# Fourier mixing and a low-rank mixer MLP on one core: wider x-stationary products on four column tiles, loads without overlap, low-rank rows by products of their own

## The chip, the core and the metric

The kernel runs on one core of a Trainium2 chip. The metric is the device time of one execution in microseconds. Six runs of the kernel before gave a median of 494.63 us (490.86 to 497.08). The engines are named as in the profile: PE (matmul; PEld is its weight load), DVE (vector), ACT (scalar), POOL (GpSimd), SP (the engine that issues most DMAs).

## The reference

The input `x` has 8 sequences of 3136 rows of 256 numbers. The real part of a two-dimensional Fourier transform (over the rows and over the 256 columns) goes into a mixer layer:

```python
X = np.fft.fft(np.fft.fft(x, axis=1), axis=2).real
xt = X.transpose(0, 2, 1)
h = xt @ U @ V                      # U: 3136 x 32, V: 32 x 3136
u = X + h.transpose(0, 2, 1)
out = u + np.maximum(u @ w_ch1, 0.0) @ w_ch2    # 256 -> 1024 -> 256
```

## The kernel before

The 3136 rows are factored as 49 x 64 (`N1`, `N2`), so the row transform has a 49-point stage and a 64-point stage; by symmetry 25 of the 49 frequencies (`NK1`) are computed. The transform of the 256 columns is folded into the weights (`W1p`, `W1m`, `W2`, `Bp`, `Bm`) and into sums and differences of mirrored columns. The eight sequences run as four pairs.

**The first pair** is treated apart. Its two sequences are loaded one at a time by `load_single` (L108), as bf16, into one tile `X` of 98 partitions x 32 lines x 256 columns: odd partitions hold lines 33 to 63, even partitions the lines 31 down to 0. The pool of that tile has a single buffer, so the second sequence cannot be loaded before the last product of the first has read it. Line 32 goes to `x32`. The last of the big loads (two rows, issued at L124) writes a row that the loads of L121 and L122 have also written; the framework therefore makes POOL wait for those loads before it issues this one and everything behind it on its queue.

The 49-point stage with x stationary is `turned_products` (L206). For each of 128 column pairs (d and 256-d) and for each of the two line halves c (lines 0 to 31 of one kind and of the other) it loads a 98 x 32 slice of `X` as weights and streams 50 columns of the table `Fs`. The four outputs of a step lie on four column tiles (32 partitions each): two columns d and 64+d, two halves. `turned_out` (L225) copies PSUM to the tile `g` with one instruction of 63 partitions for each column half h. `line32` and `row32` add row 63 by a DMA from a small tile. The framework keeps order between all writes into `g`, so the copies of DVE and ACT run one after another. For the first sequence this happens in four rounds of 16 columns (L581 to L584, PSUM pool `psh`), for the second in eight steps of 8 columns (`turned_steps`, PSUM pool `psd` of two buffers) that lie among the MLP's work.

**Low-rank part.** `te_single` (L278) forms U^T times the row-transformed data from `g`; `te_out` casts it to the tile `te`, and `spread` copies `te` into partitions 64 to 127 of `g` for every one of the 25 frequencies. The 64-point stage `s3_steps` (L299) then multiplies `g` (128 partitions: 64 of data, 64 of low-rank rows) with the table `T`, whose partitions 64 to 127 hold V and a mirrored V; it writes `q`.

**Front.** Before the first product, tables are made: index patterns on POOL (iotas), angles on DVE, sines on ACT. T's row 63 comes by a DMA from `trow` (L452), which POOL fills; the mirror copy of T (L576) waits for it, and it stands ahead of the `g` copies on DVE. The tables `residual_tables` (L409) are made on DVE ahead of `te_out`. `keep_warm` runs matmuls on zeros.

**The MLP.** A chunk is up to 512 tokens; there are 13 a pair, with 4 slots each. In a slot PE runs `mlp1` of the current chunk (two 128-wide hidden blocks, 4 matmuls of 512 columns into one PSUM tile of `psh`), ACT turns it to bf16 with a relu (hT, L360), PE runs `mlp2` of the chunk before (8 matmuls L369 and 2 L372). Every second slot ACT copies half of the output (om, L378), DVE makes sum and difference (L379, L380) and SP issues four output DMAs (L384). `plan` (L676) places all other work by hand in these slots: the first sequence's remaining `s3` steps in slots 1 to 8, the second sequence's turned steps in slots 4 to 11, its `te_single` in slot 15, the next pair's loads from slot 8 on. [...]

Of the kernel before, what the change touches and what calls it, by code (L numbers as in the profile page):

```python
# [22 lines left out]
def kernel(  # L23
# [84 lines left out]
    def load_single(b):  # L108

        X = zpool.tile([P, 32, D], BF16, tag="z", name="X")  # L110
        nc.vector.memset(X[0:PR, 31, :].bitcast(FP32), 0.0)
        nc.vector.memset(x32[b][:].bitcast(FP32), 0.0)
        yield X
        r0, L = b * N1, N1 - 1

        def rows(lo, n, line, step, o):
            src = bass.AP(x.tensor, x.offset + ((r0 + lo) * N2 + line) * D, [[N2 * D, n], [step * D, o.shape[1]], [1, D]])
            nc.gpsimd.dma_start(out=o, in_=src)

        rows(0, L, 33, 1, X[1:2 * L:2, 0:31, :])  # L120
        rows(0, L, 31, -1, X[0:2 * L:2, 0:16, :])  # L121
        rows(0, L, 15, -1, X[0:2 * L:2, 16:32, :])  # L122
        rows(L, 1, 33, 1, X[PR - 1:PR, 0:31, :])
        rows(L - 1, 2, 31, -1, X[PR - 4:PR:2, 0:32, :])  # L124
        nc.gpsimd.dma_start(out=x32[b][0:PR:2], in_=x_pn[r0:r0 + N1, 32, :])

# [79 lines left out]
    def turned_products(X, ps, i0, n):  # L206

        for i in range(n):
            if i % 8 == 0:
                first = [True] * 4  # L210
            for m in range(2):
                for h in range(2):
                    d = 64 * h + i0 + i
                    for c in range(2):
                        o = ps[64 * h + 32 * c:64 * h + 32 * c + 32, i]
                        w = X[0:PR, :, (256 - d if d else 128) if m else d]
                        if d:
                            f = Fs[:, 0:3:2 if m else 1, c, 0:NK1] if m else Fs[:, 0:2, c, 0:NK1]
                            oc = o[:, :, 0:NK1]
                        else:  # L220
                            f, oc = Fs[:, 0, c, 0:NK1], o[:, m, 0:NK1]
                        nc.tensor.matmul(oc, w, f, start=first[2 * h + c], stop=True, skip_group_check=True)  # L222
                        first[2 * h + c] = False

    def turned_out(g, ps, i0, n, evacs):  # L225
        for h in range(2):
            d0 = 64 * h + i0
            evacs[h](g[0:63].rearrange("p k (s d) -> p s k d", s=2)[:, :, :, d0:d0 + n],
                     ps[64 * h:64 * h + 63].rearrange("p i s k -> p s k i")[:, :, 0:NK1, :])

    def turned_steps(pr, b, X, evacs):
# [3 lines left out]
        def step(r):  # L235
            if r == 0:
                row32(g, line32(b))
            ps = psd.tile([P, 8, 2, 32], FP32, tag="ps", name="ps")
            turned_products(X, ps, 8 * r, 8)
            turned_out(g, ps, 8 * r, 8, evacs)  # L240
# [58 lines left out]
    def s3_steps(pr, b, evac):  # L299
# [4 lines left out]
        def mm(o, k1, blk, st):  # L304
            lt = pr.g[b][:, k1, blk::2]
            r = T[:, k1, 0:64] if k1 == 0 else T[:, k1, :].rearrange("p (s j) -> p s j", s=2)
            nc.tensor.matmul(o, lt, r, start=st, stop=True, skip_group_check=True)  # L307

        def step(g, blk):
            ps = psd.tile([P, 2, 256], FP32, tag="ps", name="ps")  # L310
            k0 = 4 * g
            for u in range(4):
                us = slice(u * 64, (u + 1) * 64)
                mm(ps[:, 0, us] if k0 + u == 0 else ps[:, :, us], k0 + u, blk, u == 0)
# [15 lines left out]

        for g in range(6):
# [30 lines left out]
    def mlp2(ch, t):  # L362
        q, nt = ch.pr.q, len(ch.units) // 2
        if t % 2 == 0:
            ch.po = pso.tile([P, 2, 2, P], FP32, tag="o", name="ops")
        ps = ch.po[:, t % 2]
        tk = slice(ch.c0 + t * P, ch.c0 + (t + 1) * P)
        for j in range(JT):
            nc.tensor.matmul(ps, ch.h[:, j, t * P:(t + 1) * P], W2[:, j, :], start=(j == 0 and t % 2 == 0),  # L369
                             stop=(j == JT - 1), skip_group_check=True)  # L370
# [3 lines left out]
        if t % 2 == 1 or t == nt - 1:  # L374
            n = t % 2 + 1
# [5 lines left out]
            for i in range(n):  # L381
                for hf in range(2):
                    b, r0 = ch.units[2 * (t - n + 1 + i) + hf]
                    nc.sync.dma_start(out=out[b].rearrange("(k2 k1) d -> k1 k2 d", k1=N1)[r0],  # L384
                                      in_=ob[hf * 64:(hf + 1) * 64, i])


# [47 lines left out]
    X0 = next(loads)  # L435
    for _ in loads:
# [8 lines left out]
    nc.gpsimd.dma_start(out=w2_f, in_=moe_w_ch2.rearrange("(t p) (s d) -> p t s d", p=P, s=2))  # L445
    for te in tes:
        nc.gpsimd.memset(te[64:128].bitcast(FP32), 0.0)
    trow = tmp([1, NK1, 64], "trow", BF16)
    nc.gpsimd.memset(trow[:], 1.0)
    nc.gpsimd.memset(trow[:, 0::2, 1::2], -1.0)  # L450
    nc.gpsimd.memset(trow[:, 1::2, 0::2], -1.0)
    nc.sync.dma_start(out=T[63:64, :, 0:64], in_=trow[:])  # L452

    Vk = uv.rearrange("p (k2 k1) -> p k1 k2", k1=N1)
    for lo, hi in [(0, 9), (9, 17), (17, NK1)]:
        nc.gpsimd.tensor_copy(T[64:96, lo:hi, 0:64], Vk[64:96, lo:hi, :])

# [23 lines left out]

    pv = tmp([PR, 10], "pv")
    h = ph[0:PR]
    u, m = tmp([PR, 1], "u"), tmp([PR, 1], "m")
    ts(u[:], pf[0:PR], h, 0.5 / 49, AL.subtract, AL.mult)
    ts(pv[:, 0:1], u[:], alt[0:PR, 0:1], None)
    nc.vector.scalar_tensor_tensor(pv[:, 0:1], h, 48.0 / 49, pv[:, 0:1], op0=AL.mult, op1=AL.add)
    for i, off in enumerate([192.0, 192.25, 192.5, 192.75]):
        ts(pv[:, 1 + i:2 + i], h, (0.5 if i < 2 else -0.5), off)
    ans = tmp([PR, 3, 2, 32], "ans")  # L490
    for tab, c, off in [(0, 0, 192.25), (0, 1, 192.5), (1, 0, 1), (1, 1, 2), (2, 0, 3), (2, 1, 4)]:
        ts(ans[:, tab, c, :], jf[0:PR, 0:32], pv[:, 0:1], off if off > 100 else pv[:, off:off + 1])
    mask_bits(ans[:], 16)
    sin_of(Fs[:], ans[:], 16)
    ts(m[:], h, -1.0, 1.0)
    ts(pv[:, 6:7], u[:], 24.0 / 49, m[:], AL.subtract, AL.mult)
    an2 = tmp([PR, 3, 32], "an2")
    for i, off in enumerate([0.25, 0.0, 0.5]):
        ts(pv[:, 7 + i:8 + i], m[:], off, 192.0)
        ts(an2[:, i], jf[0:PR, 0:32], pv[:, 6:7], pv[:, 7 + i:8 + i])  # L500
    mask_bits(an2[:], 16)

    ub = tmp([64, N1, R], "ub", BF16)
    nc.scalar.copy(ub[:].rearrange("p k r -> p (k r)"), U_f)
# [15 lines left out]
    mask_bits(ta[:], 18)  # L522
    ups = psh.tile([P, 2, 512], FP32, tag="h", name="ups")
# [7 lines left out]
    ua = tmp([64, NK1, 64], "ua", FP16)  # L531
    sin_of(F32[:], an2[:], 16)

# [7 lines left out]
    mask_bits(jq[:], 16)  # L543

    sin_of(ua[:], ta[:], 18)
    ts(rv[:, :, :, 1, :], ups_v, -1.0, None)
    pn = tmp([64, 2], "pn")
    ts(pn[:, 1:2], pf[0:64], 32.0, 32.0, AL.is_ge, AL.mult)
    ts(pn[:, 0:1], pn[:, 1:2], pf[0:64], 31.0, AL.subtract, AL.add)
    ts(pn[:, 0:1], pn[:, 0:1], 1.0 / S, None)  # L550
    ts(pn[:, 1:2], pn[:, 1:2], -0.25 / 32, 32.25)
    ta2 = kio.bitcast(FP32)
    ts(ta2, kio, pn[:, 0:1], pn[:, 1:2])
    mask_bits(ta2, 18)
    keep_warm(8)

    for k0, k1 in [(0, 16), (16, 25)]:
        ps = psh.tile([P, 16, 64], FP32, tag="h", name="uups")
        for k in range(k0, k1):
            o = ps[0:64, k - k0]  # L560
            nc.tensor.matmul(o, ua[:, k], ub[:, k].unsqueeze(1).to_broadcast([64, 2, R]),
                             start=((k - k0) % 8 == 0), stop=True, skip_group_check=True)
# [4 lines left out]
        if k0:  # L567
            copy_dve(us[:, k0:k1].rearrange("p k (r s) -> p k s r", s=2), ps[0:64, 0:k1 - k0].rearrange("p k (s r) -> p k s r", s=2))
        else:
            copy_act(us[:, k0:k1].rearrange("p k (r s) -> p k s r", s=2), ps[0:64, 0:k1 - k0].rearrange("p k (s r) -> p k s r", s=2))  # L570
    keep_warm(8)
    sin_of(T[0:63, :, 0:64], ta2[0:63], 18)
    Q = tmp([P, 3, P], "Q", FP32R)
    sin_of(Q[:, 0:2], jq[:], 16)
    nc.scalar.mul(Q[:, 2], Q[:, 1], -1.0)
    nc.vector.tensor_copy(T[0:64, :, 64:128], T[0:64, :, 63::-1])  # L576
# [3 lines left out]
    row32(g0, line32(0))  # L580
    for r in range(4):  # L581
        ps = psh.tile([P, 16, 2, 32], FP32, tag="h", name="tps")
        turned_products(X0, ps, 16 * r, 16)
        turned_out(g0, ps, 16 * r, 16, [copy_dve, copy_act])  # L584
    nc.scalar.copy(T[64:96, 1:9, 64:128], Vk[64:96, 48:40:-1, :])
    nc.vector.tensor_copy(T[96:128, 0:9, 0:64], T[64:96, 0:9, 0:64])
    ts(T[96:128, 1:9, 64:128], T[64:96, 1:9, 64:128], -1.0, None)
    nc.scalar.copy(T[64:96, 9:NK1, 64:128], Vk[64:96, 40:24:-1, :])

    for c in range(2):  # L590
        cs = slice(c * 512, (c + 1) * 512)
        ps = psh.tile([P, 2, 512], FP32, tag="h", name="w1ps")
        for blk in range(2):
            for f in range(2):
# [168 lines left out]
```

## Time and profile before

| quantity | value |
|---|---|
| median of six runs | 494.63 us |
| the profiled execution: its time | 497.14 us |
| the profiled execution: its span | 495.4 us |
| PE busy | 447.8 us (90%) |
| ACT, DVE, POOL busy | 290.6, 224.4, 135.3 us |
| PE busy in 0 to 100 us | 67.4 us |
| PE busy in 100 to 480 us | 372.5 us |
| mean granted PE clock | 0.959 |

The span is the time between the first and the last event of the execution; its device time is 1.74 us longer. A busy time is the time in which an engine has an instruction in work. The table's last rows split PE's busy time: after 100 us PE is hardly ever idle, in the first 100 us it is idle a third of the time.

### The profile page before, as it was taken

The numbers are of one execution on the slowest core, as the hardware profiler recorded it, in microseconds if no ns is written. First come the engines' busy times: TensorE is split into PE (matmuls) and PEld (weight loads), VectorE is DVE, ScalarE is ACT, GpSimd is POOL, SyncE is SP. The second block draws the span as 40 slices with busy tenths as digits, with TensorE's granted clock in tenths as the row PEclk, the third lists the DMA queues.
The fourth block names the chain that finished last, engine by engine and source line by source line (L and its number), as shares of the span: only waits on it lengthen the run. The fifth ranks groups of instructions, "written<-read, shape, count | busy, mean of one in ns | idle before, by whom it ended". The sixth has DMA issues, their size and how long they took to land.

```text
span 495.4 us, 11419 instructions
## 1 busy us (share of the span) xinstructions
PE 447.8 (90%) x4651; PEld 323.3 (65%) x4715; DVE 224.4 (45%) x524; ACT 290.6 (59%) x394; POOL 135.3 (27%) x134
## 2 busy tenths in 40 slices
PE   5655658999999999999999999999999999999993
PEld 2454346766778577777677777776777677766763
DVE  8326413548744353764624437645444344221211
ACT  4315514556775655677765556777746555666661
POOL 2720214358431502644306025336040000000000
PEclk9857958999999999999999999999999999999998
DMA  9430804446765935568649345767493333333423
GB/s 155 108 110 1 124 9 127 127 120 197 223 176 150 193 105 160 152 182 239 184 121 218 80 105 163 214 186 223 111 179 92 66 68 67 69 75 66 95 48 81
DMA packets 59506, 64.02 MB, mean 129 GB/s; under 512 B 13764, under 2 KB 52510, under 8 KB 59326
## 3 DMA queue, kind: packets, MB, share of 16 engines
q1 hardware_dynamic: 49086, 41.61, 36.2%
q0 software_dynamic: 8208, 15.38, 12.9%
q10 hardware_dynamic: 2160, 6.29, 3.4%
q8 instruction: 37, 0.61, 0.5%
q14 instruction: 15, 0.12, 0.1%
HBM read 34.28 MB, written 32.19 MB: 134 GB/s over the span
## 4 chain that ended last, share of the span: by engine, by line
PE 71%; DMA 7%; DVE 7%; issue 4%; ACT 3%; SPq 1%; POOL 1%; DVEq 0%; POOLq 0%; ACTq 0%
PE ops L369 29%; PE hps L358 28%; PE ops L372 4%; PE ps L307 3%; PE ps L222 2%; PE ps L179 2%; ACT hT L360 2%; DMA X<-in_x_dram 2%; DMA xa<-in_x_dram 1%; DMA g<-zturn 1%; DVE q L80 1%; DMA out_dram<-ob 1%; PE teps L269 1%; DMA T<-trow 1%; SPq L384 1%
## 5 line engine op out<-in xcount | busy, mean ns | idle before, releaser
L360 ACT ACTIVATE hT<-hps 128x1024 bf16<-128x1024 f32 (+1 forms) x208 | 202.6, 975 | 127.3 <-PE hps L358 117.8
L369 PE MATMUL ops<-W,hT 128*128 128x256 bf16 x1568 | 226.2, 274 | 1.3 <-DVE W L635 1.1
L369 PEld LDWEIGHTS <-hT 128*128 128x128 bf16 x1568 | 146.0, 98 | 35.1 <-issue 0.6
L379 DVE TENSOR_TENSOR ob<-ops,om 128x256 f32<-128x256 f32 (+1 forms) x100 | 41.9, 419 | 190.5 <-ACT om L378 179.1
L358 PE MATMUL hps<-q,W1p 128*128 128x512 bf16 (+1 forms) x416 | 104.5, 361 | 3.1 <-issue 1.4
L358 PE MATMUL hps<-q,W1m 128*128 128x512 bf16 x353 | 95.6, 379 | 2.0 <-ACT hT L360 0.5
L138 POOL TENSOR_TENSOR y<-xa,xb 98x1020 f32<-98x1020 f32 (+1 forms) x24 | 55.1, 2294 | 122.5 <-DMA xa<-in_x_dram 119.9
L80 DVE CAST q<-ps 128x512 bf16<-128x512 f32 (+3 forms) x120 | 64.5, 559 | 30.4 <-PE ps L307 26.4
L358 PEld LDWEIGHTS <-W1p 128*128 128x128 bf16 x448 | 40.7, 99 | 28.2 <-issue 3.8
L372 PEld LDWEIGHTS <-q 128*128 128x128 bf16 x392 | 38.6, 98 | 22.4 <-issue 2.0
L358 PEld LDWEIGHTS <-W1m 128*128 128x128 bf16 x384 | 35.6, 97 | 26.4 <-issue 1.4
L307 PE MATMUL ps<-T,g 128*128 128x128 bf16 (+1 forms) x400 | 38.0, 222 | 6.3 <-DVE g L291 4.3
L378 ACT COPY om<-ops 128x256 f32<-128x256 f32 (+1 forms) x100 | 36.9, 369 | 9.1 <-PE ops L369 8.5
L380 DVE TENSOR_TENSOR ob<-ops,om 128x256 f32<-128x256 f32 (+1 forms) x100 | 40.9, 409 | 0.0
L372 PE MATMUL ops<-Bp,q 128*128 128x128 f16 x200 | 38.9, 221 | 0.0
L307 PEld LDWEIGHTS <-g 128*128 128x128 bf16 x400 | 30.1, 100 | 11.8 <-DVE g L291 4.5
L372 PE MATMUL ops<-Bm,q 128*128 128x128 f16 x192 | 36.9, 219 | 0.0
L291 POOL COPY g<-te 64x1024 int32<-64x1024 int32 (+1 forms) x21 | 22.5, 1117 | 51.1 <-DVE te L255 45.2
L77 ACT CAST z<-ps 128x512 bf16<-128x512 f32 x48 | 28.2, 588 | 11.0 <-PE ps L179 10.4
L222 PEld LDWEIGHTS <-X 98*32 98x32 bf16 x1024 | 19.9, 172 | 10.8 <-issue 10.4
L103 POOL DMA_INDIRECT xb<-in_x_dram,idx x24 | 24.8, 1033 | 5.4 <-issue 4.5
L129 DVE TENSOR_TENSOR yb<-y 98x508 bf16<-98x508 f32 (+1 forms) x24 | 25.2, 1051 | 0.6 <-POOL y L138 0.6
(132 smaller groups left out, 231.3 us busy)
## 6 DMA issues: line engine op xcount, KB each, us to landing
out_dram<-ob SPq DMA_DIRECT2D x392, 64.0 KB
xa<-in_x_dram SPq DMA_DIRECT2D x24, 392.0 KB
g<-zturn SPq DMA_DIRECT2D x6, 800.0 KB
zturn<-z ACTq DMA_DIRECT2D x9, 512.0 KB
w_f<-in_moe_w_ch_dram POOLq DMA_DIRECT2D x2, 1024.0 KB, 9.3
X<-in_x_dram POOLq DMA_DIRECT2D x4, 384.0 KB, 10.7
X<-in_x_dram POOLq DMA_DIRECT2D x2, 744.0 KB, 8.0
zturn<-z ACTq DMA_DIRECT2D x3, 448.0 KB
```

The costliest lines, as they stand in the source:

```text
L77: nc.scalar.copy(o, i)
L80: nc.vector.tensor_copy(o, i)
L138: nc.gpsimd.tensor_tensor(ck.y[:, 0:n, 1:256], ck.xa[:, 0:n, 1:256], rb[:, :, 255:0:-1], op=AL.add)
L222: nc.tensor.matmul(oc, w, f, start=first[2 * h + c], stop=True, skip_group_check=True)
L307: nc.tensor.matmul(o, lt, r, start=st, stop=True, skip_group_check=True)
L358: nc.tensor.matmul(ps[:, i, 0:n], (W1p if ch.sg > 0 else W1m)[:, blk, j], q[:, blk, c0:c0 + n], start=(blk == 0), stop=(blk == 1))
L360: nc.scalar.activation(ch.h[:, 2 * jp:2 * jp + 2, 0:n], ps[:, :, 0:n], AF.Relu)
L369: nc.tensor.matmul(ps, ch.h[:, j, t * P:(t + 1) * P], W2[:, j, :], start=(j == 0 and t % 2 == 0), stop=(j == JT - 1), skip_group_check=True)
L372: nc.tensor.matmul(ps[:, j], q[:, j, tk], (Bp if ch.sg > 0 else Bm)[:, j], start=False, stop=False, skip_group_check=True)
L378: nc.scalar.copy(om[:, 0:n], ch.po[:, 0:n, 1])
L379: nc.vector.tensor_tensor(ob[:, 0:n, 0:P], ch.po[:, 0:n, 0], om[:, 0:n], op=AL.add)
L380: nc.vector.tensor_tensor(ob[:, 0:n, P:D], ch.po[:, 0:n, 0], om[:, 0:n], op=AL.subtract)
```

## The change

It has six parts.

1. `load_single`: each row of `X` is written by one load only. Two loads of one row each take the place of the single-row load and the two-row load, and `x32` is issued second.
2. The front is put in another order: the angles of `ua` first, then `Fs`, T, `F32`, `Q`; trow by two int32 fills; the mirrored V rows of T by POOL (L491) instead of ACT; the U products in four groups in the PSUM pool `pso`.
3. `turned_products` becomes `quarter_products`: one product with N=100 holds both halves c, on four column tiles that belong to four columns d, 32+d, 64+d, 96+d. `quarter_out` copies each column tile and each half apart, so a PSUM tile takes eight copies, shared in turn by ACT and DVE. The first sequence uses it for 32 of its 128 column pairs, and `half_products` and `half_out` (the old form) in rounds of 8 columns for the rest. The second sequence uses it in all of its eight steps, which move from slots 4 to 11 to slots 6 to 13.
4. The load of the second sequence is issued right after the first sequence's products, ahead of `W1p`, `te_single` and the first `s3` steps.
5. First sequence: the first four `s3` groups multiply only 64 rows of `g`, and the low-rank rows are added by further products with `te` (memset to 128 rows) as weights; `spread` is left to frequencies 8 to 24. `residual_tables` comes after the groups.
6. The last chunk: each token block gets its own PSUM tile and copies, and a part of the output DMAs is issued on ACT's queue.

```diff
-        rows(0, L, 33, 1, X[1:2 * L:2, 0:31, :])
-        rows(0, L, 31, -1, X[0:2 * L:2, 0:16, :])
-        rows(0, L, 15, -1, X[0:2 * L:2, 16:32, :])
-        rows(L, 1, 33, 1, X[PR - 1:PR, 0:31, :])
-        rows(L - 1, 2, 31, -1, X[PR - 4:PR:2, 0:32, :])
-        nc.gpsimd.dma_start(out=x32[b][0:PR:2], in_=x_pn[r0:r0 + N1, 32, :])
+        rows(33, 1, X[1:2 * L:2, 0:31, :])
+        nc.gpsimd.dma_start(out=x32[b][0:PR:2], in_=x_pn[r0:r0 + N1, 32, :])
+        rows(31, -1, X[0:2 * L:2, 0:16, :])
+        rows(15, -1, X[0:2 * L:2, 16:32, :])
+        nc.gpsimd.dma_start(out=X[PR - 1:PR, 0:31, :], in_=x_pn[r0 + L:r0 + N1, 33:64, :])
+        nc.gpsimd.dma_start(out=X[PR - 2:PR - 1, 31::-1, :], in_=x_pn[r0 + L:r0 + N1, 0:32, :])
...
+    def quarter_products(X, ps, i0, n):
+        for i in range(n):
+            for m in range(2):
+                for q in range(4):
+                    d = 32 * q + i0 + i
+                    o = ps[32 * q:32 * q + 32, i]
+                    w = X[0:PR, :, (256 - d if d else 128) if m else d]
+                    if d:
+                        f, oc = Fs[:, 0:3:2 if m else 1, :, 0:NK1] if m else Fs[:, 0:2, :, 0:NK1], o[:, :, :, 0:NK1]
...
+                    nc.tensor.matmul(oc, w, f, start=(i % 4 == 0 and m == 0), stop=True, skip_group_check=True)
+
+    def quarter_out(g, ps, i0, n, evac):
+        for q in range(4):
+            d0 = 32 * q + i0
+            for c in range(2):
+                r = 32 - c
+                evac(g[32 * c:32 * c + r].rearrange("p k (s d) -> p s k d", s=2)[:, :, :, d0:d0 + n],
+                     ps[32 * q:32 * q + r, 0:n, :, c, 0:NK1].rearrange("p i s k -> p s k i"))
...
-            ps = psd.tile([P, 8, 2, 32], FP32, tag="ps", name="ps")
-            turned_products(X, ps, 8 * r, 8)
-            turned_out(g, ps, 8 * r, 8, evacs)
+            ps = psd.tile([P, 4, 2, 2, 32], FP32, tag="ps", name="ps")
+            quarter_products(X, ps, 4 * r, 4)
+            quarter_out(g, ps, 4 * r, 4, evac)
...
+    for r in range(2):
+        ps = psh.tile([P, 8, 2, 2, 32], FP32, tag="h", name="tps")
+        quarter_products(X0, ps, 8 * r, 8)
+        quarter_out(g0, ps, 8 * r, 8, copy_alt)
     for r in range(4):
-        ps = psh.tile([P, 16, 2, 32], FP32, tag="h", name="tps")
-        turned_products(X0, ps, 16 * r, 16)
-        turned_out(g0, ps, 16 * r, 16, [copy_dve, copy_act])
+        i0 = 16 + 32 * (r // 2) + 8 * (r % 2)
...
+        half_products(X0, ps, i0, 8)
+        half_out(g0, ps, i0, 8, [copy_dve, copy_act])
...
+    for ps, (g, blk) in zip(pss, groups):
+        lines(ps, g, blk, 64)
+    for ps, (g, blk) in zip(pss, groups):
+        lines(ps, g, blk, P, tes[0])
+        move(ps, g, blk)
+    spread([(nc.vector, 8, 16)])(g0, tes[0])
...
-            place(turned_steps(cur, 1, X1, [copy_act, copy_dve]), 4, 12)
+            place(turned_steps(cur, 1, X1, copy_alt), 6, 14)
...
+            if not last or t == 0:
+                for i in range(n):
+                    for hf in range(2):
+                        store(i, hf, nc.sync)
+            else:
+                store(0, 0, nc.sync)
+                late.append(lambda: store(0, 1, nc.scalar))
+            while last and late and (t == 1 or t == nt - 1):
+                late.pop(0)()
```

## The prediction

> **What bounds the kernel now.** I read the page's slices first, then busy time by stretches, then the chain of waits, and last the timeline by engine. The stretches (length, then busy PE, PEld, DVE, ACT, POOL, clock, DMA):
>
> ```profile
> 0.00:100.00 100.00, 67.42 (x1358) 47.64 (x1369) 44.52 (x125) 41.10 (x55) 30.79 (x47) 0.81 0.44 95
> 100.00:480.00 380.00, 372.53 (x3228) 269.58 (x3280) 176.84 (x391) 245.67 (x333) 104.54 (x88) 1.00 0.56 140
> ```
>
> From 100 us to 480 us PE is 98% busy at full clock: only work taken off PE would count there, and the change takes none. So the time is to be won or lost in the first 100 us and in the tail. The chain of waits (start, duration, what) shows the two large holes of the front:
>
> ```profile
> 24.50 5.17 DMA T<-trow
> ...
> 29.77 0.58 DVE T L576
> 30.35 0.90 DVE g L80
> 31.28 0.83 ACT g L77
> 32.15 2.54 PE tps L222 x114
> ...
> 52.29 0.53 POOL X L118
> 52.82 7.92 DMA X<-in_x_dram
> 60.74 2.62 issue
> 63.37 0.67 POOL X L118
> 64.04 3.13 DMA x<-in_x_dram
> ```
>
> In the first, PE waits from 27.0 to 32.15 for a copy of g, because DVE stands at T's mirror copy, and that for the trow DMA. In the second, PE waits from 58.9 to 67.2 (8.3 us) for the second sequence: its load starts at 52.3, POOL waits at the overlapping row, and only then x32 is issued. The timeline shows one turned step (ACT, DVE, PE):
>
> ```profile
> 87.95 0.48 ACT L77 CAST g<-ps 63x400 bf16<-63x400 f32 x1 [1.08 <-PE ps L222]
> 88.46 0.58 DVE L80 CAST g<-ps 63x400 bf16<-63x400 f32 x1
> 88.89 1.03 ACT L360 ACTIVATE hT<-hps 128x1024 bf16<-128x1024 f32 x1 [0.46 <-PE hps L358]
> 89.77 1.38 PE L222 MATMUL ps<-Fs,X 98*32 98x50 f16 x64
> ```
>
> DVE starts 0.03 us after ACT's end, although both halves were in PSUM at the same time. The waits answer says the same:
>
> ```profile
> DVE g L80 <- ACT g L77: 18.3, 7, 11.9
> ```
>
> So copies into g run in a chain across the two engines. The tail's copies:
>
> ```profile
> 487.95 0.37 ACT L378 COPY om<-ops 128x256 f32<-128x256 f32 x1 [1.60 <-PE ops L369]
> 488.35 0.42 DVE L379 TENSOR_TENSOR ob<-ops,om 128x256 f32<-128x256 f32 x1 [1.21 <-ACT om L378]
> ```
>
> PE ends at 487.88; SP issues its last 12 output DMAs from 485.19 without a gap to 492.92, 0.64 us each, so the tail ends on SP's queue.
>
> [...] a step has 1.3 us of products and 1.06 us of copies. [...] Here 64 products of N=50 took 1.31 us on the chain (20.5 ns each at full clock), and in 32.15 to 37.41 about 19 ns at clock 0.5; [...] The trace's number is used. [...] I leave 20 ns[...]. [...]
>
> **The change part by part.**
>
> *Load of the first sequence.* POOL no longer waits 11.34 us (the wait ahead of the row at 15.53), so the iota of 1.58 us, V, W1, W2 and trow move up. W2's issue still waits for the first X load (landing 9.5 us after 1.42). Then two fills of 0.5 us: trow is issued at about 13 instead of 24.5 us. W1 and W2 still share the DMA engines, so I keep its 5.17 us: landed at 18.1 (from 15, with 2 us, to 20.5, when W2's bytes are through). Sines and angles are all done by 16. But the U products now lie ahead of the X products on PE, in four groups over the two buffers of pso, and the second group's copy is on DVE behind T's mirror copy: 18.15+0.58, fill 0.17, copy 0.55: 19.4. The fourth group takes 0.4, keep_warm's 8 at 0.2 to 0.43 take about 2.9: the first X product starts at S=22.7, where before it started at 19.6. S is 20.5 to 25 by trow's landing.
>
> *Copies of the first sequence.* Two tiles of 64 products (1.3 us each) come first, with 8 copies of 400 elements each. One pair in the chain costs 0.48+0.57+0.06=1.11, eight pairs 8.9. Four rounds of the old form follow; the second waits for psd (line 32 holds the other buffer): 1.1, then three times 1.33 of PE, then 1.1. Sum: S+1.3+8.9+1.1+4.0+1.1=S+16.4, or 39.1; before, g was full at 39.27. Nothing is won: the time gained on trow's wait goes into smaller copies.
>
> *From g to the first hidden activation.* w1ps 2.9 us on PE to 40.9 (X's products end at 38.0), teps 1.6 to 42.5, te copies 0.6, 64-row products 4x0.43 at cold clock, low-rank products 4x0.43 with copies behind them: q is full at 47.1. On DVE then spread 0.7, T 0.8, residual_tables 2.2 (all as in the trace): 50.8. Bp (0.5) stands ahead of the first hT on ACT: hT starts at 51.3; before, at 51.16. The five us of T, tables and spread that lay ahead of s3 have been moved behind q and are late again at Bp. W2's fold (2.4 us of DVE) is behind them: the first mlp2 at 58.1 instead of 57.6.
>
> *Load of the second sequence.* It starts at 39 (end of the g copies), six issues of 0.65, landed by about 50 to 51. The steps that need it begin at slot 6. The 8.3 us wait is gone; slot 6's hT comes at about 62.3 (58.1, two mlp2 of 1.0, two mlp1 of 0.9, small waits).
>
> *Turned steps, slots 6 to 13.* PE: 32 products of about 20 ns instead of 64, 0.65 us saved a step, 5.2 in all. Copies: 8 of 200 elements instead of 2 of 400. The trace has none of this size. Without any fixed part a copy would take half of 0.48 and 0.58 (0.24, 0.29); if all were fixed, the whole. [...] I take 0.31 and 0.36; te's casts of 129 columns from PSUM (0.29 on DVE) stand near them. The built order has every copy wait for the other engine's last one, so ACT is held for 4x0.31+3x0.36+6x0.035=2.53 us a step, in order ahead of the next hT. A slot then takes ACT 1.03 (hT)+2.53=3.56; in odd slots also om 0.39 and the chain's DVE behind the ob pair, 0.46: 4.41. PE needs 0.86+1.0+0.65=2.5 and waits. Eight slots: 4x3.56+4x4.41=31.9. Extras: q and z32 in slot 6 1.0, q in slot 7 0.7, W1m and Bm in slot 8 1.7, the pair tables in slot 10 1.1: 4.4. So slot 14's hT is at 62.3+36.3=98.6; before it was at 102.40. Gain 3.8: of the 8.3 us wait and 5.2 us of products, more than half is given back as PE waiting for ACT.
>
> *After slot 14.* The same work in the same order on a PE that is full: 0. The next pair's loads keep their slots, and slots 8 to 13 got longer, so DMA isn't later.
>
> *Tail.* The last chunk's SP issues fall from 8 to 5, with the previous chunk's 4 ahead: 485.19+9x0.64=490.95 instead of 492.92. ACT's three are done by 489.6. Gain 2.0 (1 to 2.5).
>
> **Sum.** -0 -3.8 -2.0 = -5.8: span 495.4-5.8=489.6, and 491.3 with the 1.74 us around it. The profiled execution (497.14) was 2.5 slower than the median of the runs; from the median 494.63 I forecast 488.8. Its own range: S from -2.2 to +2.5, chain links 10% either way (3 us), tail 1: 483 to 494.
>
> **The rivals.**
>
> *PE stays the bound in the turned steps.* If the chain were not kept (copies of ACT and DVE side by side) or its links were half as long, slots 6 to 13 take PE's 2.5 us plus the s3 products: about 22 instead of 36.3 us. The gain is 14 more: about 475. For it: ACT was idle half of this stage (17.6 us busy in 37.2 us). Against: the 0.03 us handover, seven times.
>
> *The copies don't shrink (slower).* If a copy of 200 elements on 32 partitions costs as much as one of 400, 0.48 and 0.58, ACT is held 4x0.48+3x0.58+0.2=3.87 a step, and the eight slots take 8x(1.03+0.2+0.23+3.87)+4.4=47. Slot 14 is at 109.4, +7.0, less the tail's 2.0: +5.0, or 499.6. It decides from an average slot of 5.26 us on, where the gains are used up ((102.4+2.0-62.3)/8); I have 4.54. For it: a 1-column DVE operation already takes 0.15 and a 98x32 one 0.20 to 0.33. Against: te's 0.29.
>
> A smaller doubt: PE, with 2.5 us of work in 4 us, may lose its clock. Before, at 43% busy (80.8 to 83.3), it was granted 0.70 in the stretch after. [...] At half clock PE needs about 4.4 us a slot, near ACT's 4.5; that costs up to 4 us, inside my range.
>
> **How the numbers follow.** Forecast 0.62, PE-bound 0.20, copies that don't shrink 0.18. A measurement here tells about 0.5%, or 2.5 us, from no change. Faster by more: 0.8 of the forecast's, all of the second: 0.70. Within: 0.17 of the forecast's and 0.2 of the third: 0.14. Slower: 0.16. The range takes half of each rival: 477 to 497.
>
> **What would show it.** Right: eight ACT-DVE pairs a step at 0.03 us handover, ACT copies near 0.31 and DVE near 0.36, PE idle before mlp1 in slots 7 to 13 and slot distance near 4.5 us; no X wait of PE after 58 us; first hT within 2 us of 51; SP's last issue near 2 us after ACT's. Wrong: a first X product before 20 us, products of N=100 near 40 ns each [...], or a hole after 100 us that wasn't there.

## The result and the profile after

The changed kernel takes 490.36 us (median of 21 runs, 487.84 to 492.1) against 494.3 us for the kernel before on the same chips (42 runs, 490.11 to 497.22): a ratio of 0.9923, 95% interval 0.9906 to 0.9941. That is 3.8 us, or 0.8%: small, but clear of no change. The two profiled spans stand further apart, 489.1 against 495.4 us, because the profiled execution before (497.14 us) lay 2.8 us over its median and the one after (490.88 us) 0.5 us over.

Busy time by stretches, in the same columns as before (length; busy PE, PEld, DVE, ACT, POOL with instruction counts; clock; DMA share; GB/s):

```profile
0.00:100.00 100.00, 63.68 (x1042) 42.07 (x1053) 56.06 (x157) 47.84 (x90) 34.04 (x51) 0.88 0.45 98
100.00:480.00 380.00, 372.19 (x3214) 269.75 (x3263) 175.23 (x392) 246.46 (x335) 103.47 (x86) 1.00 0.57 140
```

After 100 us nothing has changed for PE: 98% busy, as before. In the first 100 us PE is busy less (63.68 us, before 67.42) and idle more, while DVE is busy 11.5 us more and ACT 6.7 us. PE runs 1042 instructions there instead of 1358, DVE 157 instead of 125, ACT 90 instead of 55: the products became fewer, the copies more.

The chain of waits of the changed kernel through the front (start, duration, what):

```profile
15.24 1.70 DVE jq L439 x4
16.96 1.10 DVE jq L428
18.09 0.52 ACT Q L432
...
18.94 0.55 ACT us L77
...
20.37 0.58 ACT us L77
...
22.55 2.77 PE warm L499 x6
25.32 1.13 PE tps L217 x63
26.47 0.49 ACT g L77
26.99 0.57 DVE g L80
...
50.54 0.35 DVE qa L439
...
50.97 0.26 DVE qa L428
...
51.43 0.23 issue
51.67 1.01 ACT hT L381
```

Neither hole of the chain before is there any more, neither the wait of T's copy for trow nor the wait for the second sequence. The new limits are mostly copies and tables: DVE's angles for Q (`jq`), ACT's `us` copies queued behind Q, then the copy pairs into `g`, then the tables of `residual_tables` (`qa`), behind which Bp and the first hidden activation stand on ACT:

```profile
51.25 0.51 ACT L432 ACTIVATE Bp<-qa,pi 128x256 f16<-128x256 int32 x1 [5.00 <-DVE qa L428]
```

That first hT starts at 51.67, before at 51.16. The chain contains no waiting for X.

One of the eight steps in the timeline, as it was shown before:

```profile
90.27 0.32 ACT L77 CAST g<-ps 32x200 bf16<-32x200 f32 x1 [0.42 <-DVE g L80]
...
90.62 0.36 DVE L80 CAST g<-ps 31x200 bf16<-31x200 f32 x1 [0.38 <-ACT g L77]
91.01 0.32 ACT L77 CAST g<-ps 32x200 bf16<-32x200 f32 x1 [0.43 <-DVE g L80]
91.36 1.02 ACT L381 ACTIVATE hT<-hps 128x1024 bf16<-128x1024 f32 x1
91.36 0.37 DVE L80 CAST g<-ps 31x200 bf16<-31x200 f32 x1 [0.39 <-ACT g L77]
91.79 0.71 PE L217 MATMUL ps<-Fs,X 98*32 98x100 f16 x32 [0.69 <-DVE g L80]
92.43 1.03 PE L379 MATMUL hps<-q,W1m 128*128 128x512 bf16 x4
```

The 32 products with N=100 need 0.71 us, half of the 1.38 us that 64 products with N=50 needed. But hT stands on ACT behind the last of its four copies and starts when that ends, 1.2 us after its own products (at 90.1). Each of those copies waits for DVE's copy before it, and PE then waits for a copy too (0.69 us). Over slots 6 to 13 PE is busy 24.5 of 36.35 us. The waits say the same of the whole run (waiting engine and tile, releaser: us in total, times, longest us):

```profile
ACT g L77 <- DVE g L80: 23.3, 35, 1.7
DVE g L80 <- ACT g L77: 18.0, 32, 4.6
```

Before, the second of the two had 18.3 us in 7 times, and the first 12.7 us in 3 times, none of them in the steps. The waits in number went from 10 to 67. The tail in the timeline:

```profile
478.83 7.83 SPq L405 DMA_DIRECT2D out_dram<-ob  x10
...
483.20 0.82 PE L390 MATMUL ops<-W,hT 128*128 128x256 bf16 x6
...
484.61 1.13 ACTq L405 DMA_DIRECT2D out_dram<-ob  x2
```

PE ends at 484.0 and SP's last issue at 486.7; the span ends 5.1 us after PE, where before it ended 7.5 us after it. Counted from the last hT, which takes in the small waits that PE now has in the tail, it is 10.6 us to the end instead of 12.4.

### The profile page after: what moved, and what is told of

The parts are those of the page before. It is cut to its first block, busy times and chain, and to the rows that moved or that the text cites. A ratio compares the mean times of both kernels' runs of the same rounds, so it can differ in the third digit from the quotient of the medians.

```text
span 489.1 us, 10763 instructions
## 1 busy us (share of the span) xinstructions
PE 439.6 (90%) x4280; PEld 314.5 (64%) x4343; DVE 234.0 (48%) x558; ACT 295.4 (60%) x428; POOL 137.5 (28%) x137
## 3 DMA queue, kind: packets, MB, share of 16 engines
q1 hardware_dynamic: 48846, 41.42, 36.7%
## 4 chain that ended last, share of the span: by engine, by line
PE 69%; DVE 13%; ACT 8%; DMA 5%; issue 3%; SPq 1%; DVEq 0%; ACTq 0%
PE ops L390 28%; PE hps L379 27%; PE ps L321 4%; ACT hT L381 4%; PE ops L393 4%; DMA out_dram<-ob 3%; DVE g L80 3%; ACT g L77 2%; PE ps L178 2%; DMA g<-zturn 2%; DVE q L80 2%; SPq L405 1%; DVE ob L401 1%; PE teps L283 1%; DVE ob L400 1%
## 5 line engine op out<-in xcount | busy, mean ns | idle before, releaser
L390 PE MATMUL ops<-W,hT 128*128 128x256 bf16 x1568 | 225.3, 273 | 4.1 <-ACT hT L381 2.8
L390 PEld LDWEIGHTS <-hT 128*128 128x128 bf16 x1568 | 145.3, 98 | 38.2 <-ACT hT L381 3.0
L305 POOL COPY g<-te 64x1024 int32<-64x1024 int32 (+1 forms) x22 | 23.7, 1122 | 60.4 <-DVE te L269 47.4
L321 PE MATMUL ps<-T,g 128*128 128x128 bf16 (+3 forms) x400 | 37.5, 220 | 1.6 <-DMA g<-zturn 0.7
L77 ACT CAST z<-ps 128x512 bf16<-128x512 f32 x48 | 28.2, 587 | 10.6 <-PE ps L178 9.3
L321 PEld LDWEIGHTS <-g 128*128 128x128 bf16 (+1 forms) x400 | 29.7, 99 | 6.8 <-issue 2.0
L128 DVE TENSOR_TENSOR yb<-y 98x508 bf16<-98x508 f32 (+1 forms) x24 | 24.0, 999 | 0.0
L178 PE MATMUL ps<-yb,F 98*128 98x258 bf16 (+1 forms) x108 | 18.9, 265 | 3.0 <-DVE q L80 3.0
```

The source lines that it names most:

```text
L77: nc.scalar.copy(o, i)
L178: nc.tensor.matmul(o[..., cs], F[:, 2 * t + i].rearrange("p b k c -> p (b k c)"), y[..., cs], start=first, stop=True, skip_group_check=True)
```

## The experiments

Each kernel is the changed one with one edit, if nothing else is said. Ratios are to the kernel before, which ran on the same chip with each. The experiments ran on three chips, and the kernel before had medians of 495.62, 494.55 and 492.26 us there; to compare a ratio with the changed kernel's 0.9923 is to take it that both kernels differ alike from chip to chip. Times within the trace are of one profiled execution each; "slot 6 to 14" is the distance of the hT starts of these slots.

| kernel | median us | ratio, 95% interval | first X product | first hT | slot 6 to 14 | span |
|---|---|---|---|---|---|---|
| kernel before | 494.3 | 1 | 19.61 | 51.16 | | 495.4 |
| changed kernel | 490.36 | 0.9923 (0.9906 to 0.9941) | 25.25 | 51.67 | 36.3 | 489.1 |
| steps in the old form | 484.18 | 0.9779 (0.9745 to 0.9814) | 25.27 | 52.08 | 30.9 | 484.0 |
| the steps' copies on DVE alone | 485.47 | 0.9817 (0.9778 to 0.9857) | 23.69 | 50.94 | 28.6 | 482.8 |
| first sequence in the old form | 490.27 | 0.9886 (0.9847 to 0.9925) | 27.03 | 52.06 | 36.4 | 488.9 |
| Bp in slot 3 | 489.67 | 0.9880 (0.9844 to 0.9917) | 24.59 | 48.98 | 36.6 | 488.1 |
| old tail | 492.88 | 0.9952 (0.9931 to 0.9972) | 26.25 | 53.09 | 36.7 | 493.1 |
| load of the second sequence late | 491.67 | 0.9943 (0.9916 to 0.9970) | 23.64 | 50.98 | 36.5 | 488.8 |
| old overlapping loads | 499.21 | 1.0159 (1.0131 to 1.0187) | 33.48 | 60.94 | 36.4 | 496.1 |
| te spread instead of own products | 493.07 | 1.0001 (0.9981 to 1.0021) | 27.02 | 53.96 | 36.3 | 493.1 |
| V casts held back | 488.92 | 0.9893 (0.9848 to 0.9937) | 22.77 | 50.24 | 36.4 | 486.8 |
| three edits together | 479.39 | 0.9755 (0.9727 to 0.9782) | 23.81 | 48.29 | 27.5 | 477.9 |
| four edits together | 476.86 | 0.9713 (0.9675 to 0.9752) | 24.75 | 47.88 | 27.5 | 478.2 |
| before, with the new steps | 499.34 | 1.0107 (1.0062 to 1.0152) | 19.15 | 48.94 | | 496.3 |

The columns of the first X product and the first hT vary without an edit that could move them. The kernel before and the kernel before with the new steps have one and the same front, and their first hT differ by 2.2 us. The two traces part at the first sequence's load: POOL waits 11.34 us at the overlapping row in one and 9.07 in the other, and trow is issued at 24.50 and at 22.27.

### The steps in their old form

```diff
-            ps = psd.tile([P, 4, 2, 2, 32], FP32, tag="ps", name="ps")
-            quarter_products(X, ps, 4 * r, 4)
-            quarter_out(g, ps, 4 * r, 4, evac)
+            ps = psd.tile([P, 8, 2, 32], FP32, tag="ps", name="ps")
+            turned_products(X, ps, 8 * r, 8)
+            turned_out(g, ps, 8 * r, 8, [copy_act, copy_dve])
```

> The changed kernel, with the second sequence's eight steps (slots 6 to 13) in the old form: 64 products of N=50 and two copies of 63 partitions a step, all else as changed. If the chain of eight copies holds ACT and so sets the slot (4.54 us), slots fall to about 3.3 us, as before, and slot 14 comes 8 to 10 us earlier: about 481 us against 490.4 of the changed kernel. If instead PE sets the slots and the halved products are what the change gains, the old form costs 8 x 0.65 = 5.2 us: about 495.5.

The kernel is 1.4% faster than the changed one. Slots 6 to 14 take 30.9 us instead of 36.3, although PE has 64 products a step again instead of 32. A step in its timeline:

```profile
82.36 1.04 PE L404 MATMUL hps<-q,W1p 128*128 128x512 bf16 x4
82.48 0.49 ACT L77 CAST g<-ps 63x400 bf16<-63x400 f32 x1 [0.96 <-PE ps L261]
83.00 0.58 DVE L80 CAST g<-ps 63x400 bf16<-63x400 f32 x1 [0.70 <-ACT g L77]
...
83.44 1.03 ACT L406 ACTIVATE hT<-hps 128x1024 bf16<-128x1024 f32 x1 [0.47 <-PE hps L404]
...
84.32 1.37 PE L261 MATMUL ps<-Fs,X 98*32 98x50 f16 x64
```

ACT is done with its one copy long before PE has finished `mlp1`; hT now waits for PE (0.47 us), not for a copy. From slot 7 on a slot took 3.2 to 5.8 us; the longest lies where PE ran at clock 0.60 (70 to 74 us), the last five took 3.2 to 3.5 us. The old form is the better one: its 0.65 us more of products a step cost less than the six extra copies.

### The eight copies on one engine

```diff
-            place(turned_steps(cur, 1, X1, copy_alt), 6, 14)
+            place(turned_steps(cur, 1, X1, copy_dve), 6, 14)
```

> The changed kernel, with all eight copies of a step of the second sequence on DVE instead of in turn on ACT and DVE. If the hold of ACT by the chain sets the slot, ACT is free, DVE has 8 x 0.36 = 2.9 us and 0.4 to 0.8 us of other work a slot, and a slot takes about 3.6 instead of 4.5 us: 6 to 7 us less, about 484. If the length of the copies one after another sets it, whoever makes them, it stays at 2.9 us plus DVE's own work, and nothing is gained: 490 or a little more.

```profile
85.18 5.97 DVE L80 CAST g<-ps 32x200 bf16<-32x200 f32 x16
```

Sixteen copies without a gap in 5.97 us are 0.37 us each, eight in 2.97 us; the changed kernel needs 2.5 us of chain on ACT for the same data. Slots 6 to 14 shrink to 28.6 us, or 3.57 a slot, although the copies of a step now take longer, because ACT, which hT needs, is free. So it is not the number of copies as such but that they hold the engine of hT. Behind slot 14 DVE is the late one (`te_single` waits for its last copies at 94.85), and a part is given back: slot 14 is 9.2 us earlier than in the changed kernel, the span 6.3.

### The first sequence in its old form

All 128 column pairs in eight rounds of 8 columns, two copies of 400 elements each, over the three PSUM pools. In the changed kernel 64 of the 128 pairs, not 32, are in the wide form: two rounds of 32.

```diff
-    for r in range(2):
-        ps = psh.tile([P, 8, 2, 2, 32], FP32, tag="h", name="tps")
-        quarter_products(X0, ps, 8 * r, 8)
-        quarter_out(g0, ps, 8 * r, 8, copy_alt)
-    for r in range(4):
...
+    for r in range(8):
+        pl_, tg_ = [(psh, "h"), (psd, "ps"), (pso, "o"), (psh, "h")][r // 2]
+        ps = pl_.tile([P, 8, 2, 32], FP32, tag=tg_, name="tps")
+        turned_products(X0, ps, 8 * r, 8)
+        turned_out(g0, ps, 8 * r, 8, [copy_dve, copy_act])
```

> The changed kernel, with all of the first sequence's products in the old form, in eight rounds of 8 columns, each with two copies of 63 partitions. Theory: the sixteen small copies (8.9 us) set when g is full; without them PE's eight rounds of 1.3 us do, g is full about 3.5 us earlier and so is the first hT (48 instead of 51.7): 487. Rival: something else behind (Bp, the fold of W2, the second sequence's load) sets the MLP's start, and the time stays at 490 within 1 us.

From the first X product to the full g it takes 12.7 us instead of 15.6, the 2.9 that were expected. But the first product came at 27.03, not at 25.25, and w1ps, which follows, took 3.54 us on PE instead of 2.13. The first hT is no earlier (52.06), and the interval of the ratio overlaps that of the changed kernel: the time is the rival's. What moved the first product lies ahead of the edit; the experiment with the V casts deals with it. The longer w1ps goes with PE's granted clock, 0.56 while it ran, against 1.00 in the changed kernel.

### Bp made later

```diff
     bp_sin = residual_tables()
-    bp_sin()
...
+            place([bp_sin], 3, 4)
```

> The changed kernel, with the sine of Bp on ACT moved from ahead of the first hT to slot 3. Theory: Bp, which waits for DVE's residual tables, holds the first hT from about 48.5 to 51.7; without it the first hT comes 3 us earlier, of which the fold of W2 behind it takes part of the gain: 2 to 3 us less, about 488. Rival: the first mlp2 waits for the fold of W2 and that for DVE's tables, so the earlier hT is idle again at slot 4: no change, 490.

The first hT comes at 48.98, 2.7 us earlier, and slot 14 at 96.71, 2.4 us earlier. At slot 17 it is 4.1 us (101.56 against 105.63), at slot 19 only 1.8 us, and the span gains 1.0 us. Slot 17 gives back 0.6 us, where PE waits 2.06 us for a copy of DVE. Slot 18 gives back 1.7 us: from 106.4 to 109 us PE is busy throughout, but its granted clock is 0.50, and six matmuls L390 take 1.49 us instead of 0.82:

```profile
106.53 1.49 PE L390 MATMUL ops<-W,hT 128*128 128x256 bf16 x6
```

At the same time DVE forms the next pair's sums beside POOL:

```profile
105.82 2.48 POOL L137 TENSOR_TENSOR y<-xa,xb 98x1020 f32<-98x1020 f32 x1
```

```profile
106.02 2.83 DVE L129 TENSOR_TENSOR yb<-y 98x508 bf16<-98x508 f32 x1
```

This DVE instruction takes 0.68 us where POOL is idle. But no wait of PE for it shows here, and the changed kernel has such a meeting too (2.21 us at 108.94), so it is not what this edit loses. By the ratio the gain can't be told from none.

### The old tail

```diff
-mlp2(prv, t, i == len(chunks))
+mlp2(prv, t)
```

> The changed kernel with the last chunk's output in the old form (two token blocks together, all eight DMAs of the chunk on SP). Theory: SP's queue of 12 issues ends the run, and the change takes 2.0 us off it: about 492.4 against 490.4, with about 7.5 us from PE's last product to the end instead of 5.3. Rival: the landing of the last bytes ends it whoever issues, and the time stays at 490.4.

The ratio rises by 0.0029, or 1.4 us (the medians differ by 2.5). The two intervals overlap, so the times alone don't settle it. The traces do: SP issues to the end again, and from the last hT to the end it is 12.3 us, against 10.6 in the changed kernel and 12.4 in the one before. The tail is worth 1.7 us, near what it was costed at.

### The second sequence's load behind Bp

```diff
-    loads = load_single(1)
-    X1 = next(loads)
-    for _ in loads:
-        pass
...
     bp_sin()
+    loads = load_single(1)
+    X1 = next(loads)
+    for _ in loads:
+        pass
```

> The changed kernel with the second sequence's load issued where it was before, behind the first s3 groups and the sine of Bp. Theory: steps in slots 6 to 13 instead of 4 to 11, and a load whose parts do not wait for each other, already hide it: it starts at about 51, lands at about 61 to 62, and line 32 is wanted at 63.9: 0 to 1 us more, 490 to 491.5. Rival: the early issue is what takes away the 8.3 us wait; then PE waits again ahead of slot 6, 4 us or more: 494 or more.

The load starts at 51.2 instead of 41.0; PE's first step of the second sequence then waits 0.52 us for X at 63.2. The ratio rises by 0.002, inside the intervals. So the early issue isn't what removed the 8.3 us wait: the load needs some 12 us to the last byte, and from 51.2 on that ends just at slot 6, two slots later than the steps began before. How much of it the later slots removed and how much the loads without overlap was not taken apart.

### The old overlapping loads

```diff
-        rows(33, 1, X[1:2 * L:2, 0:31, :])
-        nc.gpsimd.dma_start(out=x32[b][0:PR:2], in_=x_pn[r0:r0 + N1, 32, :])
...
+        rows(L, 1, 33, 1, X[PR - 1:PR, 0:31, :])
+        rows(L - 1, 2, 31, -1, X[PR - 4:PR:2, 0:32, :])
+        nc.gpsimd.dma_start(out=x32[b][0:PR:2], in_=x_pn[r0:r0 + N1, 32, :])
```

> The changed kernel with the old load_single: the two-row load that writes rows already written, x32 last. Theory (the overlap is what held POOL's queue, and what part 1 wins is the front's late trow and V): POOL waits about 11 us again ahead of the two-row load near 15, trow is issued near 24 and lands near 29.5, T's mirror copy ends near 30, the second U group's copy and the fourth group follow, and the first X product starts at 34 to 36 instead of 25.25; first hT near 60; time about 9 us longer than the changed kernel, 498 to 501, ratio near 1.01. In the second load x32 comes some 4 us later, landed near 58 to 62, hidden by the steps' place at slot 6 or at most 2 us. Rival (trow's lateness is hidden because the T copy can wait): first X product within 2 us of 25, time 489 to 492.

```profile
14.68 0.69 POOL L117 DMA_DIRECT2D X<-in_x_dram  x1 [10.51 <-DMA X<-in_x_dram]
...
21.53 0.87 SPq L483 DMA_DIRECT2D T<-trow  x1
...
28.40 0.94 DVE L588 COPY T<-T 64x1600 bf16<-64x1600 bf16 x1 [2.49 <-DMA T<-trow]
```

POOL waits 10.51 us at the row again, trow is issued 11 us later than in the changed kernel (10.5), and T's copy waits for it. The first X product comes 8.2 us later, the first hT 9.3, and the kernel is 1.6% slower than the one before. Against the changed kernel that is 11.7 us by the ratios, 8.9 by the medians and 7.0 by the spans, around the 9 that were expected. In the second load POOL waits as well, for 8.67 us up to 60.19, but slot 6 only comes at 71.15 and waits for nothing. With the new order of the front, the loads without overlap are what the whole gain stands on; without them the change loses.

### The te spread instead of own low-rank products

```diff
-    te_single(first, 0, lambda g, te: None)
+    te_single(first, 0, spread([(nc.vector, 0, 8)]))
...
     for ps, (g, blk) in zip(pss, groups):
-        lines(ps, g, blk, 64)
-    for ps, (g, blk) in zip(pss, groups):
-        lines(ps, g, blk, P, tes[0])
+        lines(ps, g, blk, P)
         move(ps, g, blk)
```

> The changed kernel without part 5's own low-rank products: te is spread into g's rows 64 to 127 for frequencies 0 to 7 on DVE (0.69 us) ahead of the first four groups, which are 128 rows again. Theory of the prediction (part 5 moves nothing that decides, Bp behind DVE's tables is what starts hT): q full within 0.5 us, DVE's tables 0 to 0.7 later, first hT 51.2 to 52.4, time 490 to 491.3. Rival (own products take the spread off the path and are worth its 0.7 us and more): first hT over 52.5, time 492 to 493.

The ratio is 0.8% above that of the changed kernel, and the intervals don't overlap: the time is the rival's. But the trace does not bear out its reason. From the first X product to the first hT it takes 26.94 us instead of 26.42, so the edit itself costs 0.5 us there. Another 1.8 us lie ahead of the edit: the first X product came at 27.02, which the next experiment explains. Up to the last hT only 0.3 us are added (2.62 us late instead of 2.29). The rest of the 4.0 us between the spans lies in the tail, where the chain runs over SP's issues and an output DMA: 12.0 us from the last hT to the end instead of 10.6. Neither stretch is touched by the edit. Whether they go with it in all 22 runs (489.79 to 495.08 us) was not settled, so what part 5 is worth stays open.

### The V casts held back

The front's DVE work had come out slower than in the kernel before. In the changed kernel POOL casts V into T in six instructions, from the moment that V has landed:

```profile
15.68 1.19 POOL L489 CAST T<-uv 32x576 bf16<-32x576 f32 x1 [4.76 <-DMA uv<-in_moe_V_dram]
16.83 1.08 POOL L491 CAST T<-uv 32x512 bf16<-32x512 f32 x1
```

```profile
15.24 1.69 DVE L439 TENSOR_SCALAR jq<-jf,pl 128x65 f32<-128x65 f32 x4
16.96 1.09 DVE L428 TENSOR_SCALAR jq<-jq 128x256 int32<-128x256 int32 x1
18.15 1.29 DVE L588 COPY T<-T 64x1600 bf16<-64x1600 bf16 x1
```

A small copy from `us` on POOL makes the casts wait for the end of the U copies:

```diff
+    gate = tmp([64, 8], "gate", BF16)
+    nc.gpsimd.tensor_copy(gate[:], us[:, NK1 - 1, 0:8])
+    for lo, hi in [(0, 9), (9, 17), (17, NK1)]:
+        nc.gpsimd.tensor_copy(T[64:96, lo:hi, 0:64], Vk[64:96, lo:hi, :])
```

> The changed kernel, with POOL's six casts of V into T made to start only when the last copy of the U products is written (a small POOL copy reads it first). In the changed kernel DVE's jq operations, its mask and T's mirror copy took 1.69, 1.09 and 1.29 us while these casts ran, against 0.74, 0.29 and 0.58 before. Theory: POOL's casts slow DVE; apart from them they take the old times, the first X product comes about 2 us earlier (23.2 instead of 25.25) and so does the first hT: about 488.5. Rival: something else slows DVE (DMA writes), the operations stay long, and the time stays at 490.4 within 1.

```profile
15.06 0.74 DVE L439 TENSOR_SCALAR jq<-jf,pl 128x65 f32<-128x65 f32 x4
15.83 0.29 DVE L428 TENSOR_SCALAR jq<-jq 128x256 int32<-128x256 int32 x1
18.27 0.58 DVE L584 COPY T<-T 64x1600 bf16<-64x1600 bf16 x1 [2.15 <-DMA T<-trow]
```

The same instructions take 0.74, 0.29 and 0.58 us instead of 1.69, 1.09 and 1.29. T's copy now waits for trow, as the prediction had it, and the first X product starts at 22.77. The rival, DMA writes, falls: while these instructions ran, the DMA engines moved 351 to 413 GB/s here and 342 to 413 in the changed kernel. The slowed `jq` mask took 1.09 us, about the length of one cast (1.08 to 1.19), as if each DVE instruction waited a cast out; what makes it wait was not shown.

This also explains why the first X product moved between kernels whose front is the same. What counts is how soon after the first `jq` the first cast starts, which follows V's landing:

| first cast after the first `jq`, us | kernels | the four `jq`, us |
|---|---|---|
| 0.15, 0.19 | te spread, first sequence in the old form | 3.45, 3.49 |
| 0.25, 0.29 | old loads, old tail | 2.55, 2.57 |
| 0.40, 0.44 | steps in the old form, changed kernel | 1.69, 1.69 |
| 0.68 and more | load late, copies on DVE, Bp in slot 3 | 0.74 |

The steps are about 0.9 us each, as if three, two, one or none of the four `jq` had met a cast.

By the ratio (0.9893) the gain can't be told from none, since the changed kernel's 0.9923 lies inside its interval; by the spans it is 2.3 us. The first X product came 2.5 us earlier, the first hT 1.4: w1ps gave 1.1 us back, 3.22 us at a granted clock of 0.63 instead of 2.13 at 1.00.

### The edits together

Steps in the old form, Bp in slot 3, V casts held back:

> The changed kernel with three edits: the second sequence's steps in the old form with two copies of 400 elements, Bp made in slot 3, and POOL's six V casts held until the U copies are done. Theory (ACT's queue bounds the turned steps, Bp and the slowed DVE bound the front; each is on the path): first X product 22.8, first hT near 47 to 48, slot 14 near 88 to 91, time 480 to 482.5. Rival (PE's lower clock after a thin stretch, or DVE later, gives the front's gain back): 483 to 485, no better than the old steps alone (484.2).

The same, and the first sequence in the old form:

> As the kernel with three edits, and the first sequence's products too in the old form (eight rounds of 8 columns, two copies each, over the PSUM pools). Theory: g full 12.7 us after the first X product instead of 15.6, first hT near 45, time 1 to 3 us shorter than with three edits: 478.5 to 481. Rival (w1ps on a cold PE, T's V rows by POOL or W2's fold take the place): equal to the three edits within 1 us.

Both beat both kernels: 2.5% and 2.9% below the kernel before. The busy time by stretches with three edits:

```profile
0.00:100.00 100.00, 77.65 (x1389) 54.58 (x1403) 56.22 (x147) 48.58 (x74) 43.05 (x58) 0.88 0.52 114
100.00:480.00 380.00, 366.34 (x3147) 265.54 (x3197) 168.78 (x388) 241.93 (x331) 95.63 (x81) 1.00 0.57 138
```

PE works 14 us more in the first 100 us than in the changed kernel, on more products and on work that was late there, and ends 11 us earlier. From slot 6 to 14 it is busy 26.2 of 27.5 us, so that here PE has become the bound. Slot 14's hT is at 86.95, against 99.15. The fourth edit brings the first hT forward by only 0.4 us, since trow landed later in that execution and w1ps took 3.78 us (3.38 with three edits); the intervals of the two overlap, so its worth stays open.

### The new steps in the kernel before

Only `quarter_products` and `quarter_out` in the second sequence's steps, which stay in slots 4 to 11.

```diff
-            turned_products(X, ps, 8 * r, 8)
-            turned_out(g, ps, 8 * r, 8, evacs)
+            quarter_products(X, ps, 4 * r, 4)
+            quarter_out(g, ps, 4 * r, 4, copy_alt)
```

> The kernel before, with part 3 of the change alone in the second sequence's steps (slots 4 to 11): 32 products of N=100 and eight copies a step. Theory (the chain of copies holds ACT): the slots grow from 3.3 to about 4.5 us, so the kernel becomes slower, by 5 to 8 us: about 500 against 494.5. Rival (PE is the bound there): 5.2 us of products are saved: about 489.

The kernel before becomes 1.1% slower. The seven slots from slot 5 to slot 12 take 32.5 us instead of 28.0, that is 4.5 us more. The wide product with its eight copies, in turn on ACT and DVE, is a loss by itself, in either kernel. Part 2, the order of the front, was not undone by itself in any experiment.

## Why the prediction was right

It said 488.8 us; measured were 490.36. The mechanism held where most of the gain was seen, in the turned steps and the tail. In the front one cost was left out, and its sum came out by luck.

| by the two profiled executions, gain in us up to | said | measured |
|---|---|---|
| first hT | -0.1 | -0.5 |
| hT of slot 14 | 3.8 | 3.25 |
| last hT | 3.8 | 4.5 |
| end | 5.8 | 6.3 |

- **The turned steps: right.** It had 36.3 us from slot 6 to slot 14, and the trace has 62.81 to 99.15. That the sum agrees to the digit is luck: slot 6 took 1.0 us more than its share, slots 7 to 13 together 1.0 us less (the four extras add up to 4.5, too, not 4.4). But the terms held one by one. The copies took 0.316 us on ACT (said: 0.31) and 0.361 on DVE (0.36), the handover 0.03, and the products 21 to 22 ns each (20). For the two copy times the trace of before had no measurement; te's casts of 129 columns, with 0.29 us, were all that the prediction has beside them. PE idled, though ahead of `mlp1` only twice (2.0 and 1.5 us); oftener it waited with the step's products for a PSUM tile to be copied. A step has four ACT-DVE pairs; the eight of the prediction's list of signs are the copies. From the first hT to slot 14 the gain is 3.8 us of 8.3 us of waiting and 5.2 us of products: nearly three quarters went to the copy chain. Giving the steps their old form returned 5.5 us between slots 6 and 14.
- **Why N=100 costs 21 ns.** That it costs about the 20.5 ns of N=50 was assumed and not shown: the trace of before has no product of this width. Four `mlp1` products of 512 columns took 0.86 us there, 0.42 ns a column. At that rate, as an estimate, 100 columns one product after another would need 42 ns, close to the prediction's sign of an error (40). Half of that was measured, 32 products in 0.71 us, so they overlapped. Neighbours in a step lie on different column tiles; whether that is what let them overlap was not tested.
- **The first rival, PE as bound,** fell for the changed kernel: the chain keeps its 0.03 us handover. The kernel with three edits comes nearer to it, with 27.5 us for these slots where the rival had 22.
- **The second rival, copies that don't shrink,** fell with the 0.316 and 0.361 us.
- **The front: the zero came out by luck.** It let the first X product start at 22.7, by trow's landing, and it started at 25.25. trow had landed in time; DVE's `jq` and its mask were late beside POOL's casts, and with them Q and the `us` copies on ACT, a cost that the sum left out. With the casts held back, the start is 22.77 and the wait is trow's. Against that, g was full 15.6 us later instead of 16.4, and q 6.6 us after g instead of 8.0. These errors nearly cancel, so the first hT came at 51.67, said to be 51.3. Nor is it sure that nothing was lost: another execution of the front before, in the kernel with the new steps, had its first hT at 48.94. Of "nothing is won", the old loads show what stands behind it: they alone are worth 9 us at the first hT, and the other parts of the front use it up.
- **The second sequence's load: right in effect.** No wait of PE for X came after 58 us. It was issued at 41.0, not 39 (the trace names w1ps as what POOL waited for); as the late load shows, that was of no weight.
- **PE's clock:** the steps themselves kept theirs (1.00 from 62.81 to 99.15 us), but right behind them, from 99 to 103.4 us, PE was granted 0.68. What that cost was not measured by itself, and what decides the clock was not shown; the gain did not shrink there. The 4.4 us that the prediction gives a slot at half clock are an estimate: its 0.86 us of `mlp1` and 1.0 of `mlp2` doubled, its 0.65 of products kept.
- **After slot 14: not quite zero.** The gain grows from 3.25 us to 4.5 us at the last hT, where the prediction expected no change.
- **The tail: right.** 1.8 us from the last hT to the end in the two traces (said: 2.0), 1.7 by the kernel with the old tail. SP's last issue ended 0.9 us after ACT's, not 2.

The sum of -5.8 us fits the two profiled executions (-6.3). Against the medians (-3.9) it was 1.9 us too much: the profiled execution before was a long one, 2.8 us over its median. The first hT at 48.94 in the kernel with the new steps, whose profiled execution was a short one (1.1 us under its median), points to the landing of the first load as a large part of that: 2.2 us lie there. With two executions it stays a pointer.

## What to carry to other kernels

A wider matmul can lose what it wins if its output leaves PSUM in more instructions than before; here half the products (0.71 us a step instead of 1.38) cost four times the copies, half of them on the engine that the next activation needed, and the kernel before became 1.1% slower by it. Before an edit is costed at its products, count the copies of a step, add their handovers where they write one tile (0.03 us each here), and look which engine they hold. And a load that overwrites a part of another can hold a whole queue: POOL's stood still for 10.51 us here, and without that wait gone, this change would have been a loss of 1.6%.

## What the runs showed that was not expected

- Three kinds of DVE instruction lengthened beside POOL's casts (1.08 to 1.41 us), in the worst cases to about one cast each: the `jq` mask from 0.29 to 1.09 us, four `jq` from 0.74 to as much as 3.49, T's copy from 0.58 to 1.47. A DVE sum of the next pair did so as well in the kernel with Bp in slot 3, from 0.68 to 2.83 us beside POOL's 2.48.
- A shift of 0.3 us in the start of the first cast (15.40 or 15.68) moved the first X product by 1.8 us (27.02 or 25.25); the four `jq` took 3.45 us with the one start and 1.69 with the other.
- w1ps, the same eight matmuls, took 2.13 to 2.46 us in five of the kernels with the new front and 3.05 to 3.78 us in the seven others, though nothing in it was edited. The clock that PE was granted while it ran was 1.00 to 0.85 in the five and 0.67 to 0.50 in the seven (the "cold PE" of the expectation for four edits), and time multiplied by clock is 1.9 to 2.1 us in all twelve. So 1 us or more that an edit wins ahead of w1ps can be gone behind it. What decides the clock there was not tested.
